# One two-column VectorE operation for a tile's guarded sum and the next tile's threshold, in an attention and two mixture-of-experts layers

## The chip, the cores and the metric

The kernel runs on one core of a Trainium2 chip. The metric is device microseconds of one execution. Engines are named as in the profile: PE is the matrix engine (PEld its weight loads), DVE is VectorE, ACT is ScalarE, POOL is GpSimd, SP issues most DMAs. Each engine runs its own instructions in the order in which they were written, and they meet through semaphores.

## The reference

Three layers follow each other, all in float32: an attention with a threshold (2 batches, 8 heads, 576 rows, 64 columns a head), and two mixture-of-experts layers over 1152 rows of 512, the first with 8 experts and a gate that is normalised over rows and columns in turn, the second with 4. Only the attention is touched here:

```python
scores = scale * np.matmul(q, k.transpose(0, 1, 3, 2))
thresh = np.max(scores, axis=-1, keepdims=True) - tau
scores = np.where(scores >= thresh, scores, -1000000000.0)
scores = scores - np.max(scores, axis=-1, keepdims=True)
attn = np.exp(scores)
attn = attn / (np.sum(attn, axis=-1, keepdims=True) + 1e-09)
return np.matmul(attn, v).astype(np.float32)
```

## The kernel before

The attention takes 72 tiles of 128 query rows by 576 keys, one after the other, in the first 232 us. Beside them PE computes the first two experts for the rows that are ready, matrix products written into the gaps ("fills", `expert_fill`), and ACT and POOL split their weights into a high and a low part (`cook`). The rest of the program, the other experts and the second layer, follows without a gap. A value written "fp32r" is the high or the low part of such a split.

What happens to a tile `u`, in the order of its life:

- `scores`: PE writes 128x576 scores into PSUM (`sc`, two buffers).
- `top`: DVE takes the largest of each row over the 576 (L287), 128x1, into column 0 of a small SBUF tile `st` (8 columns, six buffers); it stores the negative of it except in the first four tiles.
- `line`: the threshold, largest minus tau, into column 2. Three forms: the first four tiles do it with two DVE operations (L297, L298); the other twelve of the first sixteen (`exact`, products in full float32) with one DVE operation (L295); the remaining 56 with one ACT operation on 128x1 (L292).
- `exp`: ACT takes exp(score - largest) of the whole tile, PSUM to SBUF (L305).
- `mask`: one DVE operation multiplies by (score >= threshold) and sums the row into column 3 (L309; the sum is read out by a second short instruction).
- `guard`: DVE adds 1e-9 to the sum, 128x1 (L313).
- `norm`: DVE takes the reciprocal (L317) and POOL multiplies the tile by it in SBUF (L319).
- `turn`, `hi`, `lo`: PE transposes the tile (L327), ACT copies the high part out (L334, L336), DVE subtracts for the low part (L349, L352); then PE multiplies by v (L374, L376).

`step` writes the program. One call serves several tiles at different ages: `a` is the tile whose scores are ready, `d` the one before it, `x` one two tiles older than `d`. On DVE a step of the 56 reads: mask of `d`, top of `a`, guard of `d`, reciprocal of `d`, low part of `x`, further low parts (L401 of a finished head, L536 of a fill). On ACT: high part of `x`, exp of `a`, threshold of `a`, then the fill's activation (L533) and splits. So the threshold of `a` stands behind its exp on ACT, and the next step's mask waits for it. POOL's program has the norm of `d` (L319), the splits of keys, queries, values and finished heads (L85, L253, L254, L257) and a weight tile (L109).

The order is fixed by the program text: no scheduler moves an instruction. The number of fill products in a step is fixed too.

Of the kernel before, what the change touches and what calls it, by code (L numbers as in the profile page):

```python
# [9 lines left out]
F32 = mybir.dt.float32  # L10
F32R = mybir.dt.float32r
AF = mybir.ActivationFunctionType
ALU = mybir.AluOpType
AX = mybir.AxisListType
# [5 lines left out]
P = 128  # L20
# [3 lines left out]
HS = S // 2  # L24
# [5 lines left out]
def attention_two_moe_kernel(ctx, tc, qP, kP, qT, kT, vp, tau, wg, w1, w1s, w2, w2s, dp, m2w1s, m2w2, m2w2s, out):  # L30
    nc = tc.nc
    V, A, G, T = nc.vector, nc.scalar, nc.gpsimd, nc.tensor
# [24 lines left out]
    esc = cp.tile([P, 1], F32, name="esc")  # L57
    lin = cp.tile([P, 2], F32, name="lin")
    on = cp.tile([P, 2], F32, name="on")
# [32 lines left out]
    def fetch(n):  # L92
        while len(raws) < n and tiles:
            w, e, ft = tiles.pop(0)
            raw = rp.tile([P, DM], F32, tag="raw", name="raw", bufs=3)
            nc.sync.dma_start(raw, w[e, :, ft])
            raws.append(raw)
# [16 lines left out]
    class Expert:  # L114


        def __init__(self, i):
            self.w1 = lambda ft: cooked[2 * FT * i + ft]
            self.w2 = lambda ft: cooked[2 * FT * i + FT + ft]


    class Attention:
# [5 lines left out]
        def __init__(self, pl, ps_s, ps_t, ps_r, ps_m):  # L128
            self.pl, self.ps_s, self.ps_t, self.ps_r, self.ps_m = pl, ps_s, ps_t, ps_r, ps_m
            self.units, self.heads = [], []  # L130
            self.t = -2
            self.work = {}
            self.later, self.late = [], []
            self.iq = self.iv = self.lq = self.lv = 0
            self.xf = {}
            self.eth = pl.tile([P, 5, 640], F32R, name="eth")
            self.e32 = pl.tile([P, 5, 512], F32, tag="etl", name="e32")
            self.etl = None
            self.qz = [pl.tile([P, 3 * D], F32R, name=f"qz{i}") for i in range(2)]
            for z in self.qz:  # L140
                V.tensor_scalar(z[:, D:2 * D], ident[:, :D], 0.0, None, op0=ALU.mult)
# [141 lines left out]
                             start=i == 0, stop=i == len(ops) - 1)  # L283

        def top(self, u):
            st = u["st"] = self.pl.tile([P, 8], F32, tag="st", name="st", bufs=6)
            V.tensor_reduce(st[:, 0:1], u["sc"][:, :, :HS], axis=AX.XY, op=ALU.max, negate=not u["q"][0][0]["ws"])  # L287

        def line(self, u):
            st = u["st"]  # L290
            if not u["q"][0][0]["exact"]:
                A.activation(st[:, 2:3], st[:, 0:1], AF.Identity, bias=on[:, 1:2], scale=-1.0)  # L292
                return
            if not u["q"][0][0]["ws"]:
                V.tensor_scalar(st[:, 2:3], st[:, 0:1], -1.0, on[:, 0:1], op0=ALU.mult, op1=ALU.subtract)  # L295
                return
            V.tensor_scalar(st[:, 1:2], st[:, 0:1], lin[:, 0:1], None, op0=ALU.mult)  # L297
            V.tensor_scalar(st[:, 2:3], st[:, 0:1], lin[:, 1:2], None, op0=ALU.subtract)  # L298

        def exp(self, u):  # L300
            ex = u["ex"] = self.pl.tile([P, 2, HS], F32, tag="ex", name="ex", bufs=4)
            if u["q"][0][0]["ws"]:
                A.activation(ex, u["sc"][:, :, :HS], AF.Exp, bias=u["st"][:, 1:2], scale=esc)
            else:
                A.activation(ex, u["sc"][:, :, :HS], AF.Exp, bias=u["st"][:, 0:1])  # L305

        def mask(self, u):
            st, ex = u["st"], u["ex"]
            V.scalar_tensor_tensor(ex, u["sc"][:, :, :HS], st[:, 2:3], ex, op0=ALU.is_ge, op1=ALU.mult,  # L309
                                   accum_out=st[:, 3:4])  # L310

        def guard(self, u):
            V.tensor_scalar(u["st"][:, 4:5], u["st"][:, 3:4], 1e-9, None, op0=ALU.add)  # L313

        def norm(self, u):
            st = u["st"]
            V.reciprocal(st[:, 5:6], st[:, 4:5])  # L317
            exf = u["exf"] = u["ex"].rearrange("p a b -> p (a b)")
            G.tensor_scalar(exf, exf, st[:, 5:6], 1.0, op0=ALU.mult, op1=ALU.mult)  # L319

        def turn(self, u):
            eg, exf = u["eg"], u["exf"]
# [94 lines left out]
        def flush(self):  # L417
            self.run(self.later)
            self.run(self.late)

        def step(self, fill, side):

            us, t = self.units, self.t
            un = lambda i: us[i] if 0 <= i < len(us) else None
            self.load()
            nxt, a, d, x, c, z, y = (un(t + i) for i in (2, 1, 0, -2, -3, -4, -5))
            if x:
                self.turn(x)
            if d:
                self.mask(d)  # L430
            if a:
                self.top(a)
            if d:
                self.guard(d)
            if a and a["q"][0][0]["exact"]:
                self.line(a)
            if d:
                self.norm(d)
            for part, u in ((2, y), (1, z), (0, c)):
                for g in u["mix"] if u else ():  # L440
                    if g["head"]["exact"]:
                        self.mix(g, part)
            end = t > len(us)
            if x and not end:
                self.hi(x)
            for u, late in ((z, False), (y, True)):
                for g in u["mix"] if u else ():
                    if late == g["head"]["exact"]:
                        self.out(g)
            if end:  # L450
                self.run(self.later)
            if x and end:
                self.hi(x)
            if a:
                self.exp(a)
                if not a["q"][0][0]["exact"]:
                    self.line(a)
            fill(0, bool(c and c["mix"]))
            if x:
                self.lo(x)  # L460
            if nxt:
                self.scores(nxt)
            self.run(self.later)
            for g in c["mix"] if c else ():
                if not g["head"]["exact"]:
                    self.mix(g, 0)
            for w in self.work.pop(t, ()):
                w()
            fill(1, bool(c and c["mix"] or z and z["mix"]))
            self.run(self.late)  # L470
            side()
            self.t += 1
            return self.t < len(us) + 5
# [111 lines left out]
    with ExitStack() as att:  # L585
# [5 lines left out]
        at = Attention(ap, ps_s, ps_t, ps_r, ps)  # L591
# [20 lines left out]
        def side():  # L612
            if at.t >= -1:
                fetch(2)
            if at.t >= nA0 - 3 and raws and room[0] and (at.t % 3 < 2 if at.t < nA1 else room[0] > 2 or at.t % 2):
                room[0] -= 1
                cook()
            if at.t == 20:
                nc.sync.dma_start(wg_sb, wg)
                nc.sync.dma_start(dp_sb, dp)  # L620
            if at.t == 24:
                split(V, V, wg2[:, :, :E1], wg2[:, :, E1:], wg_sb)
# [962 lines left out]
```

## Time and profile before

| | |
|---|---|
| time, median of 3 runs | 1287.21 us (1286.96 to 1287.28) |
| the profiled execution | 1287.24 us, of it span 1285.5 us |
| busy: PE, DVE, ACT, POOL | 1268.6, 878.0, 738.0, 897.4 us |
| attention | first 232 us of the span |

Busy time is summed over the span; in the attention the engines take turns in being the last, so the part on the change is read from that stage alone. "Idle before, releaser" behind a row is how long the engine stood idle and whose end let it go on.

### The profile page before, as it was taken

What the parts mean: (1) busy time and instruction counts of PE and PEld (TensorE: products, weight loads), DVE (VectorE), ACT (ScalarE), POOL (GpSimd) and SP (SyncE); (2) the same over time, 40 slices, a digit from 0 to 9 for tenths busy, and PEclk for the clock granted to TensorE, in tenths of its full rate; (3) what the DMA queues carried; (4) which work ended last, traced back from release to release, by engine and by line L of the source; (5) the groups of instructions that cost most, each with busy time, mean ns of one, the idle gap of its engine ahead of it and who ended that gap; (6) DMA issues with size and microseconds to landing.
All of it is one profiled execution on the core that took longest, in us unless ns stands there. A gap on an engine that the chain in (4) does not pass through costs nothing.

```text
span 1285.5 us, 25112 instructions
## 1 busy us (share of the span) xinstructions
PE 1268.6 (99%) x9373; PEld 1209.0 (94%) x9373; DVE 878.0 (68%) x1843; ACT 738.0 (57%) x1491; POOL 897.4 (70%) x987
## 2 busy tenths in 40 slices
PE   8998999999999999999999999999999999999998
PEld 5597988889889999999999999999989999999998
DVE  6798888566637666666666666666745666666667
ACT  7887887423546555554655555466546465556552
POOL 7997987415796767867676786767668578677760
PEclk9999999999999999999999999999999999999999
DMA  5542330101221112211111221111212012111102
GB/s 170 162 126 77 97 98 17 42 1 34 81 67 50 42 42 58 58 34 51 50 42 42 58 59 34 50 50 42 58 38 62 17 53 57 35 55 50 42 18 74
DMA packets 43226, 73.84 MB, mean 57 GB/s; under 512 B 5217, under 2 KB 12513, under 8 KB 43105
## 3 DMA queue, kind: packets, MB, share of 16 engines
q1 hardware_dynamic: 42816, 71.96, 19.6%
q8 instruction: 74, 1.21, 0.4%
q14 instruction: 48, 0.39, 0.1%
q10 hardware_dynamic: 288, 0.28, 0.1%
HBM read 69.86 MB, written 2.36 MB: 56 GB/s over the span
## 4 chain that ended last, share of the span: by engine, by line
PE 89%; DVE 6%; ACT 2%; POOL 1%; issue 1%; DMA 1%; SPq 0%; DVEq 0%; POOLq 0%; ACTq 0%
PE mm L1123 36%; PE mm L1435 33%; PE mm L555 5%; PE mm L527 4%; PE mm L1243 3%; PE mm L282 2%; PE mm L327 2%; DVE ex L309 1%; PE mm L367 1%; DVE st L287 1%; PE mm L376 1%; DVE etl L349 1%; PE mm L374 1%; ACT ex L305 0%; DVE hl L536 0%
## 5 line engine op out<-in xcount | busy, mean ns | idle before, releaser
L85 POOL TENSOR_TENSOR wl<-raw,wh 128x512 fp32r<-128x512 f32 x217 | 282.9, 1310 | 180.2 <-ACT wh L80 166.9
L1223 DVE SCALAR_TENSOR_TENSOR acc<-mm,p,acc 128x256 f32<-128x256 f32 (+1 forms) x428 | 195.3, 508 | 72.5 <-PE mm L1435 59.6
L1435 PE MATMUL mm<-wh,h 128*128 128x256 f32 x960 | 173.6, 280 | 0.0
L1130 ACT COPY snap<-mm 128x576 f32<-128x576 f32 x126 | 80.8, 642 | 157.4 <-DVE mm L1284 77.8
L80 ACT CAST wh<-raw 128x512 fp32r<-128x512 f32 x217 | 133.4, 627 | 47.1 <-PE mm L1435 26.4
L1435 PEld LDWEIGHTS mm<-wh,h 128*128 128x128 f32 x960 | 146.7, 188 | 0.0
L1123 PE MATMUL mm<-xh,wl 128*128 128x288 f32 x672 | 146.3, 299 | 0.3
L1123 PE MATMUL mm<-xh,wh 128*128 128x288 f32 x672 | 143.6, 295 | 0.0
L1123 PE MATMUL mm<-xl,wh 128*128 128x288 f32 x672 | 143.1, 294 | 0.0
L1435 PE MATMUL mm<-wl,h 128*128 128x256 f32 x480 | 134.8, 281 | 0.0
L1435 PE MATMUL mm<-wh,tails 128*128 128x256 f32 x696 | 126.4, 280 | 0.0
L85 POOL TENSOR_TENSOR wl<-sum,wh 128x512 fp32r<-128x512 f32 x82 | 107.0, 1305 | 8.1 <-ACT wh L80 8.1
L1123 PEld LDWEIGHTS mm<-xh,wl 128*128 128x128 f32 x672 | 106.4, 188 | 2.8 <-DVE mm L1143 0.5
L1123 PE MATMUL mm<-xth,wl 128*128 128x288 f32 x504 | 108.3, 296 | 0.1
L1123 PEld LDWEIGHTS mm<-xl,wh 128*128 128x128 f32 x672 | 107.9, 188 | 0.0
L1123 PEld LDWEIGHTS mm<-xh,wh 128*128 128x128 f32 x672 | 107.8, 188 | 0.0
L1123 PE MATMUL mm<-xtl,wh 128*128 128x288 f32 x504 | 107.8, 295 | 0.0
L1123 PE MATMUL mm<-xth,wh 128*128 128x288 f32 x504 | 107.7, 295 | 0.0
L1435 PEld LDWEIGHTS mm<-wh,tails 128*128 128x128 f32 x696 | 106.3, 188 | 0.0
L80 ACT CAST wh<-sum 128x512 fp32r<-128x512 f32 x82 | 51.5, 628 | 85.4 <-POOL sum L820 71.9
L1435 PE MATMUL mm<-wl,tails 128*128 128x256 f32 x348 | 97.4, 280 | 0.0
L1435 PEld LDWEIGHTS mm<-wl,h 128*128 128x128 f32 x480 | 90.3, 188 | 0.4
(242 smaller groups left out, 3489.5 us busy)
## 6 DMA issues: line engine op xcount, KB each, us to landing
raw<-in_w1s SPq DMA_DIRECT2D x56, 256.0 KB, 2.7
raw<-in_w2s SPq DMA_DIRECT2D x48, 256.0 KB, 2.6
raw<-in_w SPq DMA_DIRECT2D x40, 256.0 KB, 3.1
raw<-in_m2w1s SPq DMA_DIRECT2D x32, 256.0 KB, 2.7
raw<-in_m2w2s SPq DMA_DIRECT2D x28, 256.0 KB, 2.6
kr<-in_kT SPq DMA_DIRECT2D x22, 288.0 KB, 3.0
vr<-in_vp SPq DMA_DIRECT2D x24, 160.0 KB, 2.3
qr<-in_qT SPq DMA_DIRECT2D x8, 288.0 KB, 2.9
```

The lines of the kernel that those rows point to most:

```text
L80: A.copy(hi, src)
L85: el.tensor_tensor(lo, src, f(hi), op=ALU.subtract)
L282: T.matmul(sc[:m, hf, :HS], lhsT=q, rhs=kk[:, hf * HS:(hf + 1) * HS], start=i == 0, stop=i == len(ops) - 1)
L287: V.tensor_reduce(st[:, 0:1], u["sc"][:, :, :HS], axis=AX.XY, op=ALU.max, negate=not u["q"][0][0]["ws"])
L327: T.transpose(et[:, kt], exf[:, kt * P:(kt + 1) * P], ident)
L527: T.matmul(ph[:, :n], lhsT=a[:, kt * P:(kt + 1) * P], rhs=x[:, kt, n0:n0 + n], start=i == 0 and kt == 0, stop=i == 2 and kt == KT - 1)
L555: T.matmul(py, lhsT=x, rhs=a, start=i == 0, stop=i == 3 * FT - 1)
L1123: T.matmul(ch[b][:, g, :HS], lhsT=w[:, (2 * g + kt) * P:(2 * g + kt + 1) * P], rhs=operand(u, kt, lo), start=first and j == 0, stop=j == l ...
L1130: A.copy(v[u], m)
L1223: V.scalar_tensor_tensor(a, src, s, a, op0=ALU.mult, op1=ALU.add)
L1243: T.matmul(py, lhsT=hid[x][:, kk, o:o + P], rhs=w[y], start=n == 0, stop=n == 3 * HF - 1)
L1435: T.matmul(m, lhsT=hid(x, kt + ko), rhs=wk[y], start=first and n == 0, stop=n == 5, skip_group_check=True)
```

## The change

The tile `st` with its six buffers of 8 columns goes, and one tile `sums` of six slots by 8 columns comes, which a step uses by turns. Its columns are laid out so that a step's two small subtractions stand side by side: columns 0 and 1 hold the sum of `d` and the constant tau term, columns 2 and 3 hold -1e-9 and the negated largest of `a`, and one tensor_tensor subtracts the second pair from the first into columns 4 (the guarded sum) and 5 (the threshold). Column 2 is filled once by a POOL memset, column 1 once by a DVE operation in step 0. The operation takes the place of `guard` and `line` in 68 steps: the 56 in which `line` was on ACT and the 12 in which it was a second DVE operation. The first four tiles keep their two operations, and the last step has a guard alone.

```diff
+            self.sums = pl.tile([P, 6, 8], F32, name="sums")
+            G.memset(self.sums[:, :, 2], -1e-9)
...
         def top(self, u):
-            st = u["st"] = self.pl.tile([P, 8], F32, tag="st", name="st", bufs=6)
-            V.tensor_reduce(st[:, 0:1], u["sc"][:, :, :HS], axis=AX.XY, op=ALU.max, negate=not u["q"][0][0]["ws"])
+            s = self.sums[:, (self.t + 6) % 6]
+            u["max"], u["line"] = s[:, 3:4], s[:, 5:6]
+            V.tensor_reduce(u["max"], u["sc"][:, :, :HS], axis=AX.XY, op=ALU.max, negate=not u["q"][0][0]["ws"])
...
-            if not u["q"][0][0]["exact"]:
-                A.activation(st[:, 2:3], st[:, 0:1], AF.Identity, bias=on[:, 1:2], scale=-1.0)
-                return
-            if not u["q"][0][0]["ws"]:
-                V.tensor_scalar(st[:, 2:3], st[:, 0:1], -1.0, on[:, 0:1], op0=ALU.mult, op1=ALU.subtract)
-                return
...
+            else:
+                V.tensor_tensor(s[:, 4:6], s[:, 0:2], s[:, 2:4], op=ALU.subtract)
...
         def mask(self, u):
...
+            V.scalar_tensor_tensor(ex, u["sc"][:, :, :HS], u["line"], ex, op0=ALU.is_ge, op1=ALU.mult,
+                                   accum_out=self.sums[:, self.t % 6, 0:1])
-        def guard(self, u):
-            V.tensor_scalar(u["st"][:, 4:5], u["st"][:, 3:4], 1e-9, None, op0=ALU.add)
...
             if a:
                 self.top(a)
-            if d:
-                self.guard(d)
-            if a and a["q"][0][0]["exact"]:
-                self.line(a)
+            self.line(a, d)
             if d:
                 self.norm(d)
...
             if a:
                 self.exp(a)
-                if not a["q"][0][0]["exact"]:
-                    self.line(a)
...
+            if at.t == 0:
+                V.tensor_scalar(at.sums[:, :, 1], at.sums[:, :, 2], 0.0, on[:, 1:2], op0=ALU.mult, op1=ALU.add)
```

DVE's program around 100 us into the execution, before: a tile's top, the guard and reciprocal of the tile ahead of it, a low part, the mask (`mm` is PSUM, `ex` the exp tile, `etl` the low part).

```order
L287 TENSOR_REDUCE st_1349<-mm_95 128x1 [waits PE_49]
L313 TENSOR_SCALAR st_1321<-st_1321 128x1 [waits DVE_49]
L317 RECIPROCAL st_1321<-st_1321 128x1 [waits DVE_49]
L349 TENSOR_TENSOR etl_986<-mm_95,eth_113 128x4x128 [waits Activation_49]
L309 SCALAR_TENSOR_TENSOR ex_1355,st_1349<-mm_95,st_1349,ex_1355 128x576 [waits Activation_49,Pool_49]
L287 TENSOR_REDUCE st_1397<-mm_95 128x1 [waits PE_49]
```

The same place in DVE's program with the change.

```order
L290 TENSOR_REDUCE sums_115<-mm_95 128x1 [waits PE_49]
L304 TENSOR_TENSOR sums_115<-sums_115 128x2 [waits DVE_49]
L320 RECIPROCAL sums_115<-sums_115 128x1 [waits DVE_49]
L352 TENSOR_TENSOR etl_943<-mm_95,eth_113 128x4x128 [waits Activation_49]
L315 SCALAR_TENSOR_TENSOR ex_1297,sums_115<-mm_95,sums_115,ex_1297 128x576 [waits Activation_49]
L290 TENSOR_REDUCE sums_115<-mm_95 128x1 [waits PE_49]
```

No instruction changes its place on DVE; the one-column operation on the sum of the tile ahead has become a two-column one that also reads what the operation right in front of it writes, and the mask waits on one semaphore where it waited on two.

ACT's program at the same place before: two tiles' exps, each with its threshold behind it, and what stands between.

```order
L305 ACTIVATE ex_1328<-mm_95,st_1321 128x576 [waits DVE_49,Pool_49]
L292 ACTIVATE st_1321<-st_1321,on_82 128x1
L334 CAST eth_113<-mm_95 128x4x128 [waits DVE_49,PE_49]
L305 ACTIVATE ex_1355<-mm_95,st_1349 128x576 [waits DVE_49,Pool_49]
L292 ACTIVATE st_1349<-st_1349,on_82 128x1
L80 CAST vhl_1382<-vr_1066 128x5x64 [waits DMAHW7_49,Activation_49]
```

And with the change.

```order
L311 ACTIVATE ex_1272<-mm_95,sums_115 128x576 [waits DVE_49,Pool_49]
L337 CAST eth_113<-mm_95 128x4x128 [waits DVE_49,PE_49]
L311 ACTIVATE ex_1297<-mm_95,sums_115 128x576 [waits DVE_49,Pool_49]
L80 CAST vhl_1323<-vr_1021 128x5x64 [waits DMAHW7_49,Activation_49]
L80 CAST kh_1326<-kr_1168 128x576 [waits DMAHW3_49,PE_49,Activation_49]
```

The threshold is gone from ACT and nothing else has moved; PE's and POOL's programs stand as before, but for POOL's one memset ahead of the first tile.

## Rows read from the trace of the kernel before

**Rows 1.** Windows: stretch, then busy us (and count) by engine, clock, DMA share.

```profile
46.00:71.10 25.10, 24.57 (x148) 17.43 (x149) 19.97 (x55) 21.41 (x48) 24.29 (x29) 1.00 0.55 155
71.10:98.28 27.18, 25.44 (x188) 23.68 (x187) 24.61 (x64) 22.75 (x54) 25.05 (x31) 1.00 0.44 125
127.80:178.20 50.40, 50.40 (x343) 47.69 (x344) 44.29 (x113) 39.87 (x87) 45.56 (x76) 1.00 0.33 93
...
240.00:1285.40 1045.40, 1040.73 (x7927) 1016.21 (x7925) 680.90 (x1313) 549.93 (x1084) 705.90 (x730) 1.00 0.17 48
```

**Rows 2.** Waits of DVE, 46 to 232 us: us in total, times, longest.

```profile
DVE hl L536 <- ACT hh L533: 6.7, 16, 0.5
DVE ex L309 <- ACT st L292: 6.2, 17, 0.9
DVE etl L349 <- ACT eth L334: 5.9, 8, 1.2
```

**Rows 3.** Chain that ended last, in order of time: start, us, piece.

```profile
71.10 0.28 ACT st L292
...
76.76 0.17 DVE st L317
...
223.93 0.29 ACT st L292
...
228.79 0.16 DVE st L317
```

**Rows 4.** Timeline of DVE, 115 to 118 us: start, us, operation, idle before.

```profile
115.39 0.75 DVE L287 TENSOR_REDUCE st<-mm 128x1 f32<-128x576 f32 x1
116.06 0.15 DVE L313 TENSOR_SCALAR st<-st 128x1 f32<-128x1 f32 x1
116.24 0.17 DVE L317 RECIPROCAL st<-st 128x1 f32<-128x1 f32 x1
116.32 0.67 DVE L349 TENSOR_TENSOR etl<-mm,eth 128x512 fp32r<-128x512 f32 x1
117.26 0.82 DVE L309 SCALAR_TENSOR_TENSOR ex<-mm,st,ex 128x576 f32<-128x576 f32 x1 [0.27 <-ACT st L292]
```

**Rows 5.** Timeline of ACT in the same step.

```profile
116.23 0.74 ACT L305 ACTIVATE ex<-mm,st 128x576 f32<-128x576 f32 x1 [0.81 <-DVE st L313]
116.87 0.28 ACT L292 ACTIVATE st<-st,on 128x1 f32<-128x1 f32 x1
117.06 0.45 ACT L80 CAST vhl<-vr 128x320 fp32r<-128x320 f32 x1
```

**Rows 6.** Timeline of DVE, 4 to 7 us, ahead of the first tiles.

```profile
4.93 0.16 DVE L609 TENSOR_TENSOR on<-tau_sb,on 128x1 f32<-128x1 f32 x1
...
6.00 0.76 DVE L287 TENSOR_REDUCE st<-mm 128x1 f32<-128x576 f32 x1 [0.73 <-PE mm L275]
6.79 0.21 DVE L297 TENSOR_SCALAR st<-st,lin 128x1 f32<-128x1 f32 x1
```

**Rows 7.** Timelines of DVE and POOL, 281 to 291 us, after the attention.

```profile
281.54 0.45 DVE L953 TENSOR_TENSOR sums<-sums 128x288 f32<-128x288 f32 x1
...
289.60 0.93 DVE L953 TENSOR_TENSOR sums<-sums 128x288 f32<-128x288 f32 x1
...
288.92 1.29 POOL L820 TENSOR_TENSOR raw<-sum,raw 128x512 f32<-128x512 f32 x1
```

**Rows 8.** Timelines of DVE and POOL, 78 to 80 us.

```profile
78.71 0.69 DVE L85 TENSOR_TENSOR wg<-wg_sb,wg 128x32 fp32r<-128x32 f32 x1
...
78.61 0.75 POOL L319 TENSOR_SCALAR ex<-ex,st 128x576 f32<-128x576 f32 x1
```

**Rows 9.** Groups of POOL by shape, 46 to 232 us: count, busy, mean ns, idle before.

```profile
L319 POOL TENSOR_SCALAR ex<-ex,st 128x576 f32<-128x576 f32 x59 | 44.0, 747 | 10.9 <-DVE st L317 10.4 <-PE mm L282 0.3
L109 POOL TENSOR_TENSOR wl<-raw,wh 128x512 fp32r<-128x512 f32 x25 | 32.3, 1291 | 0.0
L85 POOL TENSOR_TENSOR kl<-kr,kh 128x576 fp32r<-128x576 f32 x15 | 21.4, 1428 | 4.0 <-ACT kh L80 4.0
```

More of the change, by code (lines that the diff above doesn't have):

```diff
@@ L285, in top, with line @@
         def top(self, u):
-            st = u["st"] = self.pl.tile([P, 8], F32, tag="st", name="st", bufs=6)
-            V.tensor_reduce(st[:, 0:1], u["sc"][:, :, :HS], axis=AX.XY, op=ALU.max, negate=not u["q"][0][0]["ws"])
-        def line(self, u):
-            st = u["st"]
-            if not u["q"][0][0]["exact"]:
-                A.activation(st[:, 2:3], st[:, 0:1], AF.Identity, bias=on[:, 1:2], scale=-1.0)
-                return
-            if not u["q"][0][0]["ws"]:
-                V.tensor_scalar(st[:, 2:3], st[:, 0:1], -1.0, on[:, 0:1], op0=ALU.mult, op1=ALU.subtract)
-                return
-            V.tensor_scalar(st[:, 1:2], st[:, 0:1], lin[:, 0:1], None, op0=ALU.mult)
-            V.tensor_scalar(st[:, 2:3], st[:, 0:1], lin[:, 1:2], None, op0=ALU.subtract)
+            s = self.sums[:, (self.t + 6) % 6]
+            u["max"], u["line"] = s[:, 3:4], s[:, 5:6]
+            V.tensor_reduce(u["max"], u["sc"][:, :, :HS], axis=AX.XY, op=ALU.max, negate=not u["q"][0][0]["ws"])
+        def line(self, u, d):
+            s = self.sums[:, (self.t + 6) % 6]
+            ws = u and u["q"][0][0]["ws"]
+            if ws or not u:
+                if d:
+                    V.tensor_scalar(s[:, 4:5], s[:, 0:1], 1e-9, None, op0=ALU.add)
+                if ws:
+                    u["bias"] = s[:, 7:8]
+                    V.tensor_scalar(u["bias"], u["max"], lin[:, 0:1], None, op0=ALU.mult)
+                    V.tensor_scalar(u["line"], u["max"], lin[:, 1:2], None, op0=ALU.subtract)
+            else:
+                V.tensor_tensor(s[:, 4:6], s[:, 0:2], s[:, 2:4], op=ALU.subtract)
         def exp(self, u):
@@ L302, in exp @@
             if u["q"][0][0]["ws"]:
-                A.activation(ex, u["sc"][:, :, :HS], AF.Exp, bias=u["st"][:, 1:2], scale=esc)
+                A.activation(ex, u["sc"][:, :, :HS], AF.Exp, bias=u["bias"], scale=esc)
             else:
-                A.activation(ex, u["sc"][:, :, :HS], AF.Exp, bias=u["st"][:, 0:1])
+                A.activation(ex, u["sc"][:, :, :HS], AF.Exp, bias=u["max"])
         def mask(self, u):
-            st, ex = u["st"], u["ex"]
-            V.scalar_tensor_tensor(ex, u["sc"][:, :, :HS], st[:, 2:3], ex, op0=ALU.is_ge, op1=ALU.mult,
-                                   accum_out=st[:, 3:4])
-        def guard(self, u):
-            V.tensor_scalar(u["st"][:, 4:5], u["st"][:, 3:4], 1e-9, None, op0=ALU.add)
+            ex = u["ex"]
+            V.scalar_tensor_tensor(ex, u["sc"][:, :, :HS], u["line"], ex, op0=ALU.is_ge, op1=ALU.mult,
+                                   accum_out=self.sums[:, self.t % 6, 0:1])
         def norm(self, u):
-            st = u["st"]
-            V.reciprocal(st[:, 5:6], st[:, 4:5])
+            s = self.sums[:, self.t % 6]
+            V.reciprocal(s[:, 6:7], s[:, 4:5])
             exf = u["exf"] = u["ex"].rearrange("p a b -> p (a b)")
-            G.tensor_scalar(exf, exf, st[:, 5:6], 1.0, op0=ALU.mult, op1=ALU.mult)
+            G.tensor_scalar(exf, exf, s[:, 6:7], 1.0, op0=ALU.mult, op1=ALU.mult)
         def turn(self, u):
```

## The prediction

> **What bounds the kernel now.** I read the windows first. From 240 us on PE is busy for 1040.7 of 1045.4 us [rows 1] and nothing there is edited, so whatever the attention gains or loses moves the end by as much. Inside the attention PE is full from 127.8 to 178.2 us, but from 71.1 to 98.3 us it is busy for only 25.4 of 27.2 [rows 1]: there something else paces the program. POOL is the busiest or nearly so all along: 24.3 of 25.1 us from 46 us on, then 25.1 of 27.2, then 45.6 of 50.4 [rows 1]. Next I read who DVE waits for: the mask waits 17 times for the threshold on ACT, 6.2 us, and the fill's low part L536 waits 16 times, 6.7 us, for an activation that stands behind the threshold on ACT [rows 2]. The chain of waits tells which of these cost time. Between 46 and 232 us it runs through the threshold on ACT in 14 pieces, the first at 71.1 and the last at 223.9 us, and through the reciprocal on DVE in 11, from 76.8 to 228.8 us [rows 3]. So in about 25 of the 56 steps DVE and ACT set the pace; in the 14 DVE waits for ACT, in the 11 it works without a pause. The other steps are paced by PE, or around 46 to 71 us by POOL.
>
> **What leaves ACT.** 56 thresholds of 0.28 us. The next ACT operation starts 0.19 us after the threshold, because operations overlap (116.87 to 117.06) [rows 5]. That is the gain for L536 on a chain piece. For a mask it is more: without the threshold it follows the exp, which ends at 116.97 (116.23 and 0.74), instead of 117.26 [rows 4, 5], at most 0.29. On ACT's side the 14 pieces are worth 14 x 0.19 = 2.7 us or somewhat more. ACT elsewhere has idle time, and there it is worth nothing.
>
> **What comes to DVE: the dependency.** The guard needs only the old sum, so it starts 0.67 us after the top's start, before the top ends (115.39 and 0.75 is 116.14; guard at 116.06); 0.18 later comes the reciprocal, 0.08 later the low part [rows 4]. The new operation reads the largest that the top has just written. L297 does that at the program's start: it comes 0.79 us after the top's start, 0.03 after its end [rows 6]. A tensor_tensor on one column takes 0.16 us [rows 6]; the reciprocal then comes 0.16 + 0.03 = 0.19 later. So the low part starts 0.79 + 0.19 + 0.08 = 1.06 us after the top's start, where it was 0.93: **+0.13 us** on DVE in each step.
> The Trainium skill, page VectorE: DVE Perf Modes, section The DRAIN you can't avoid, says that the next operation waits for the pipe to empty in any case and that a semaphore costs nothing on top. By that the dependency is free and the sum below is 11 x 0.13 = 1.4 us smaller. The overlap of guard and top above speaks against it, and the rows decide.
>
> **What comes to DVE: the port.** This is the larger term, and the one I chose. The guard reads one tensor. The new operation reads two, both in SBUF. No DVE operation of the attention's steps does that: mask, top and the low parts take one input from PSUM. Where the trace has such operations, they stretch while POOL runs. L953 on 288 columns takes 0.45 us at 281.54; the same one at 289.60 takes 0.93, with a POOL operation from 288.92 to 290.21 beside it, and it ends 0.32 us after that one [rows 7]. Closer to this case, a 128x32 subtraction sits once between two steps: it takes 0.69 us from 78.71 to 79.40, and POOL's norm runs from 78.61 to 79.36 [rows 8]. It seems to stand until POOL's operation is through and to end 0.04 us behind it. No row shows two columns. The bounds are nothing (it slips through, 0.16 us) and the rest of a whole POOL operation, up to 1.43 us [rows 9]. I take the nearest row, the 32 columns: blocked, and done 0.04 us after POOL.
> The Trainium skill, page SBUF — State Buffer, section Who interferes with whom, speaks against this change in so many words: a VectorE instruction with two SBUF inputs contends with a GpSimd instruction that reads SBUF, and the one that comes second is fully blocked for the whole instruction. The trace agrees for 288 and 32 columns; by that rule width does not matter, and without it the sum below is that of the first rival.
> How long is such a wait? If the operation falls at any time of the 186 us from 46 to 232, the mean rest of a POOL operation is count x duration squared / 2, over 186. The three groups of rows 9 give 59 x 0.28 + 25 x 0.83 + 15 x 1.02 = 52.6, or 0.28 us. From each wait 0.12 us goes off, as the operation would take 0.16 anyway and ends 0.04 after POOL; the groups cover 97.7 us, 0.53 of the time, so 0.22 remains. They leave out POOL's smaller instructions, and POOL is busy for 0.90 to 0.97 of the stretches [rows 1], so I take **0.30 us a step**. A step then costs DVE 0.13 + 0.30 = 0.43 us.
>
> **Sum.** (1) The 11 pieces in which DVE works without a pause: 11 x 0.43 = +4.7. (2) The 14 pieces through ACT: DVE's own path had on average 6.2 / 17 = 0.36 us of idle before the mask and 6.7 / 16 = 0.42 before L536 [rows 2]. With 0.43 more it catches up with ACT's gain: the mean of both is about zero, and because the later of two ends counts and the waits scatter, I put +0.08 each, +1.1. (3) The mask waits on one semaphore where it waited on two. It starts 0.11 us after the threshold's end [rows 4, 5], which bounds that at 0 to 0.11 on DVE's pieces; I take -0.4 in all. (4) From 46 to 71 us POOL paces the program. A blocked operation is released when POOL's ends, and if POOL's next is the norm, it stands until the reciprocal is through (0.03 + 0.16 and some): 0 to 0.28 on 8 steps, I take half, +1.2. (5) Where PE paces, some 21 steps, DVE has slack (5.9 us in eight waits for the transposes' copies [rows 2]) against 0.43 a step, less what ACT gives back: between 0 and 9, and I take +1.0, as the slack lies in few places and long waits do not fit into the others. Together +7.6.
> At nothing I cost: the 12 full-float32 tiles, where one operation takes the place of two and DVE then waits for the exp (without that cover 12 x 0.43 = 5.2); POOL's memset and DVE's one-time fill, which stand beside the wait for the first data and for an exp (0.2 us each, uncovered); and a shift of the staging tiles in SBUF by the 192 bytes of `sums`, which no row prices. No DMA and no queue of SP is moved. Behind the waiting operation on DVE stand the reciprocal, for which POOL's norm waits, and the low parts, for which PE's products wait.
> The sum is made on the profiled execution, 1287.24 us, 0.03 above the median: 1287.24 + 7.6 = **1294.8 us**.
>
> **The rivals.**
> *Not slower: two columns slip past POOL.* Then DVE's step costs 0.13: 11 x 0.13 = 1.4, less 2.7, less 0.4, is -1.7, so 1285.5 us. For it speaks that no row has an operation so short; against it that the 32 columns were held as long as any. It decides on DVE's wait: with a mean under 0.13 us a step, 11 x (0.13 + 0.13) = 2.9 is met by 2.7 and 0.4, and the kernel is not slower.
> *The wait is absorbed.* The operation is blocked, but in the first 11 pieces it mostly finds POOL between operations, or POOL and DVE fall into step: half of (1), nothing of (4) and (5): 2.4 + 1.1 - 0.4 = +3.1 at the most, +1.5 in the middle, 1288.7 us. For it: POOL waits 10.4 us for reciprocals [rows 9], where nothing of POOL is in the way. Against it: POOL's busy share.
> *DVE becomes the bound everywhere.* All 56 steps pay 0.43, less 14 x 0.36 of idle and 2.7 us that ACT gives: 24.1 - 5.0 - 2.7 = +16.4, 1303.6 us. For it: from 127.8 to 178.2 us DVE is busy for 44.3 of 50.4 us; against it, that is still 0.4 us of room a step in 15 steps.
>
> **How the numbers follow.** A measurement of this kernel tells about 0.2%, 2.6 us, from no change. Forecast 0.70, nearly all of it slower than 1289.8. Slips past: 0.13, of which 0.05 is faster than 1284.6. Absorbed: 0.10, of which 0.08 is within 0.2%. Bound everywhere: 0.07. Faster 0.05, same 0.18, slower 0.77. The range goes from 1286.0, where some 0.08 of the first rival is left below, to 1301.0, with 0.10 left above; the forecast alone spans 1290 to 1301, its terms (1), (4) and (5) at their ends.
>
> **What would show it.** In the profile after, the new 128x2 operation should have a least duration of 0.16 us and a mean near 0.45, the long ones ending just after a POOL operation; its start should be 0.79 us after the top's, against 0.67 for the guard. The mask's waits for ACT should shrink, the chain should hold more DVE and POOL than now, and PE's busy share from 71 to 98 us should fall. After 240 us all should be as before, only later. If the operation never exceeds 0.2 us, the port step is wrong and the first rival holds. If it does and the attention is not longer, the sum of (1) and (2) is wrong.

## The result and the profile after

The changed kernel takes 1298.6 us (median of 6 runs, 1297.6 to 1298.79) against 1287.11 us for the kernel before on the same chip (6 runs, 1286.89 to 1287.28): a ratio of 1.0087, 95% interval 1.0076 to 1.0098, 11.5 us slower. The forecast was 1294.8 us, 7.6 us slower, in a range of 1286.0 to 1301.0. The side was right, the size two thirds of what came. The profiled execution of after is 1298.63 us with a span of 1296.8, where the span before was 1285.5: the two traces differ by 11.3 us, and that is what has to be found.

First the page of after: busy us and share of each engine, and then the chain of waits, its shares by engine, after and, below it, before.

```profile
PE 1270.8 (98%) x9373; PEld 1208.2 (93%) x9373; DVE 904.9 (70%) x1832; ACT 729.2 (56%) x1435; POOL 897.4 (69%) x988
```

```profile
PE 82%; DVE 10%; POOL 3%; ACT 2%; issue 2%; DMA 0%; DVEq 0%; POOLq 0%; ACTq 0%
```

```profile
PE 89%; DVE 6%; ACT 2%; POOL 1%; issue 1%; DMA 1%; SPq 0%; DVEq 0%; POOLq 0%; ACTq 0%
```

DVE is busy 26.9 us longer (878.0 before), though the change gives it one operation for one in the 56 steps and one for two in the 12 full-float32 tiles; ACT is 8.8 us less busy. In the chain DVE has 10% where it had 6, POOL 3 where it had 1. Next the same stretches as in [rows 1]: busy us and count of PE, PEld, DVE, ACT, POOL, then clock and DMA.

```profile
46.00:71.10 25.10, 24.28 (x143) 16.66 (x144) 22.94 (x56) 20.49 (x41) 24.20 (x31) 1.00 0.51 149
71.10:98.28 27.18, 25.71 (x192) 24.13 (x191) 26.19 (x63) 21.41 (x46) 25.06 (x30) 1.00 0.46 130
127.80:178.20 50.40, 45.47 (x309) 41.90 (x308) 47.96 (x102) 34.74 (x68) 42.21 (x72) 1.00 0.28 85
...
250.00:1296.70 1046.70, 1041.27 (x7930) 1016.10 (x7928) 680.77 (x1313) 549.82 (x1084) 706.19 (x731) 1.00 0.17 48
```

The gap opens late. From 127.8 to 178.2 us PE, full before (50.40), is busy for 45.47 us, and DVE, which had 6 us of room, has 2.4. From 46 to 98 us DVE is busier by even more (4.6 us against 3.7), and PE loses nothing: 49.99 us in the two stretches, 50.01 before. After 250 us PE works as it did, but for about 0.8 us.

The operation that does it, over the whole span of after: group, count, then busy us, mean ns of one, idle us before it.

```profile
L304 DVE TENSOR_TENSOR sums<-sums 128x2 f32<-128x2 f32 x68 | 34.4, 505 | 2.3
```

DVE's timeline in after (start, us, operation): the fill of the constant column, one step in which the operation is free, and the longest.

```profile
9.81 1.33 DVE L614 TENSOR_SCALAR sums<-sums,on 128x6 f32<-128x6 f32 x1
...
116.51 0.75 DVE L290 TENSOR_REDUCE sums<-mm 128x1 f32<-128x576 f32 x1
117.30 0.16 DVE L304 TENSOR_TENSOR sums<-sums 128x2 f32<-128x2 f32 x1
117.49 0.17 DVE L320 RECIPROCAL sums<-sums 128x1 f32<-128x1 f32 x1
117.57 0.67 DVE L352 TENSOR_TENSOR etl<-mm,eth 128x512 fp32r<-128x512 f32 x1
...
165.12 3.39 DVE L304 TENSOR_TENSOR sums<-sums 128x2 f32<-128x2 f32 x1
168.55 0.16 DVE L320 RECIPROCAL sums<-sums 128x1 f32<-128x1 f32 x1
```

POOL's timeline beside the fill and beside the longest:

```profile
9.71 1.41 POOL L85 TENSOR_TENSOR kl<-kr,kh 128x576 fp32r<-128x576 f32 x1
...
163.86 1.30 POOL L109 TENSOR_TENSOR wl<-raw,wh 128x512 fp32r<-128x512 f32 x1
165.13 0.76 POOL L322 TENSOR_SCALAR ex<-ex,sums 128x576 f32<-128x576 f32 x1
165.84 1.43 POOL L85 TENSOR_TENSOR kl<-kr,kh 128x576 fp32r<-128x576 f32 x1
167.23 1.27 POOL L109 TENSOR_TENSOR wl<-raw,wh 128x512 fp32r<-128x512 f32 x1
168.91 0.74 POOL L322 TENSOR_SCALAR ex<-ex,sums 128x576 f32<-128x576 f32 x1 [0.41 <-DVE sums L320]
```

Alone, at 117.30, the subtraction takes 0.16 us. At 165.12 it takes 3.39: three of POOL's operations pass, and it ends at 168.51, 0.01 after the last of them (167.23 and 1.27). Of the 68, 43 take more than 0.20 us, and 42 of these end 0.01 to 0.02 us after the end of a POOL operation. That POOL is what they stand behind rests on these ends; no run here takes POOL's work away. Over their least time the 68 stand 68 x (0.505 - 0.160) = 23.5 us; I call that the hold. DVE's waits of 6.2 us for the threshold and 6.7 for the fill's activation on ACT [rows 2] are all but gone; its waits in after, 46 to 244 us (us in total, times, longest):

```profile
DVE etl L352 <- ACT eth L337: 2.9, 5, 0.9
DVE ex L315 <- ACT ex L311: 1.0, 3, 0.5
DVE hl L534 <- ACT hh L531: 0.7, 4, 0.2
```

**Where the 11.3 us come from.** A mask starts each step on DVE; the start of the n-th mask after, less that of the n-th before, is how far the program is behind. The last row puts the forecast's terms (1), (2), (4) and (5) where their pieces stood; (3), -0.4, is left out.

| mask started before at, us | 16.3 | 44.3 | 68.1 | 129.5 | 220.3 | 229.8 |
|---|---|---|---|---|---|---|
| behind, after | 0.36 | 1.16 | 0.56 | 1.21 | 10.30 | 10.00 |
| behind, by the forecast's terms | 0 | 0 | 1.2 | 4.5 | 7.1 | 8.0 |

So 9.1 us are lost between 129.5 and 220.3 us, and next to nothing from 44 to 129. The loss from there on follows, for the most part, single holds. DVE's timeline in after, two long holds ahead of 129 us and one behind it:

```profile
55.45 1.20 DVE L304 TENSOR_TENSOR sums<-sums 128x2 f32<-128x2 f32 x1
103.66 1.13 DVE L304 TENSOR_TENSOR sums<-sums 128x2 f32<-128x2 f32 x1
...
135.92 1.43 DVE L304 TENSOR_TENSOR sums<-sums 128x2 f32<-128x2 f32 x1
```

From the mask ahead of it to the mask behind it, the lag grows by 0.20 us over the first, 0.14 over the second, and 1.40 over the third. Over the longest, the 3.39 us at 165.12, it grows by 2.82, which is nearly a third of the 9.1. Most long holds behind 129 us pass on in this way, though not all: over the 1.25 us at 184.33 it grows by 0.07.

Then 0.35 more are lost until the first long run of products behind the attention, and 1.05 around 350 us, far behind the change. ACT's timeline there, in the kernel before:

```profile
349.44 0.62 ACT L80 CAST wh<-raw 128x512 fp32r<-128x512 f32 x1 [2.41 <-DMA raw<-in_w]
```

And in after:

```profile
360.99 0.62 ACT L80 CAST wh<-raw 128x512 fp32r<-128x512 f32 x1 [3.61 <-PE mm L1123]
```

This split of a weight comes 11.55 us later where its neighbours come 10.36 later, and PE then waits 0.8 us for a copy that stands behind it on ACT. Whether the weight's transfer was late or its buffer, the trace does not settle (before it names the transfer, after a product of PE). It seems not to come with the change as such: none of the traces of the twelve kernels below loses more than 0.2 us at this place. Two of the six runs of after, 1297.6 and 1297.83, are some 1 us shorter than the other four (1298.56 to 1298.79) and may be without it; they have no trace.

### The profile page after: what moved, and what is told of

The parts are those of the page before. It is cut to its first block, busy times and chain, and to the rows that moved or that the text cites. A ratio compares the mean times of both kernels' runs of the same rounds, so it can differ in the third digit from the quotient of the medians.

```text
span 1296.8 us, 25008 instructions
## 1 busy us (share of the span) xinstructions
PE 1270.8 (98%) x9373; PEld 1208.2 (93%) x9373; DVE 904.9 (70%) x1832; ACT 729.2 (56%) x1435; POOL 897.4 (69%) x988
## 3 DMA queue, kind: packets, MB, share of 16 engines
q8 instruction: 74, 1.21, 0.4%
## 4 chain that ended last, share of the span: by engine, by line
PE 82%; DVE 10%; POOL 3%; ACT 2%; issue 2%; DMA 0%; DVEq 0%; POOLq 0%; ACTq 0%
PE mm L1123 34%; PE mm L1435 33%; PE mm L553 4%; PE mm L525 4%; PE mm L1243 3%; DVE ex L315 2%; DVE sums L290 2%; DVE sums L304 1%; DVE etl L352 1%; PE mm L330 1%; PE mm L284 1%; POOL wl L85 1%; DVE hl L534 1%; ACT ex L311 1%; POOL wl L109 1%
```

## The experiments

My theory was the forecast's: the new operation reads two tensors in SBUF, for which it uses a port of POOL, and it stands while POOL works. The rivals were the dependency (guard, reciprocal and low part now wait for the largest) and simply one operation more on DVE in steps that have no room. All kernels were compared with the kernel before on the same chip, whose median over all these runs was 1286.8 to 1286.9 us.

**One input in place of two (one_in).**

```diff
-                V.tensor_tensor(s[:, 4:6], s[:, 0:2], s[:, 2:4], op=ALU.subtract)
+                V.tensor_scalar(s[:, 4:6], s[:, 0:4:3], 1e-9, None, op0=ALU.add)
```

> The changed kernel, with its two-column operation in the same place and with the same producers and consumers, but with one input tensor in SBUF (a constant is added to the sum and to the negated largest) in place of two; the thresholds that come out are not the reference's. Port theory: the operation is never held behind POOL, it takes 0.16 us each time, the 23.5 us of holding in the changed kernel's trace are gone, DVE pays 0.13 us a step for the dependency and ACT is rid of its threshold: about 1286 us (1284 to 1288). Dependency theory (the loss comes from waiting for the largest, ahead of guard, reciprocal and low part): the operation costs a step as much as before, 1294 us or more.

Measured: 1297.75 us, 1.0082 (1.0065 to 1.0099). **My theory fell**, or so it looked: with one input the operation is held just as well. Its group, 18 to 244 us:

```profile
L304 DVE TENSOR_SCALAR sums<-sums 128x2 f32<-128x2 f32 x68 | 35.0, 514 | 2.3
```

Its long cases end 0.02 to 0.04 us after a POOL operation, and the one at 165.47 takes 3.42 us.

**Two one-column operations (dve_two).**

```diff
-                V.tensor_tensor(s[:, 4:6], s[:, 0:2], s[:, 2:4], op=ALU.subtract)
+                if d:
+                    V.tensor_scalar(s[:, 4:5], s[:, 0:1], 1e-9, None, op0=ALU.add)
+                V.tensor_scalar(u["line"], u["max"], -1.0, on[:, 0:1], op0=ALU.mult, op1=ALU.subtract)
```

> The changed kernel with its two-column operation replaced by two operations of DVE on one column, each with one input tensor: guard, then threshold. The threshold has left ACT here too. Port theory: neither is held; the guard starts 0.67 us after the top again, the threshold adds some 0.2 us of DVE to a step, paid in the 25 steps or so that DVE and ACT pace, less what ACT gives back: 25 x 0.2 - 2.7 = +2.3, about 1289 us (1285 to 1291). If any threshold on DVE costs what the change cost, because DVE has no room in the steps from 128 to 224 us: 1295 us or more.

Measured: 1286.88 us, 0.9999 (0.999 to 1.0009), the time of the kernel before. So DVE does have room for the threshold. The groups of threshold and guard, 18 to 244 us:

```profile
L306 DVE TENSOR_SCALAR sums<-sums,on 128x1 f32<-128x1 f32 x68 | 14.6, 214 | 0.0
L305 DVE TENSOR_SCALAR sums<-sums 128x1 f32<-128x1 f32 x68 | 9.7, 143 | 0.0
```

Neither is ever held: the means are the least times. The reciprocal starts 0.92 us after the top's start (0.85 before, 0.97 at the least in the changed kernel), so a threshold on DVE costs 0.07 us a step, and at the last mask this kernel is 1.39 us ahead of the kernel before. That is what ACT gives back, less the 0.07 and less 0.30 lost at the start.

**An additional operation that nothing waits for (plus_tt, plus_ts).** Here the kernel before is left as it is, and one operation on a tile of its own is put behind the guard, with two inputs or with one:

```diff
+            if a and not a["q"][0][0]["exact"]:
+                V.tensor_tensor(self.pad[:, 4:6], self.pad[:, 0:2], self.pad[:, 2:4], op=ALU.subtract)
...
+                V.tensor_scalar(self.pad[:, 4:6], self.pad[:, 0:2], 1e-9, None, op0=ALU.add)
```

> The kernel before, with one more DVE operation in each of the 56 steps, behind the guard: a subtraction of two columns from two columns of a tile in SBUF that nothing else uses. Nothing waits for its result, ACT keeps its threshold. Port theory: it takes 0.16 us at least and about 0.5 us on average, the long ones end just behind a POOL operation, and the kernel is 8 to 14 us slower, 1295 to 1301 us. Dependency theory: it costs 0.16 us in the steps that DVE paces, 1289 to 1291 us.

> The same as the one with two inputs, but the additional operation adds a constant to two columns: one input tensor. Both theories: 0.15 us each, never held, at most 0.16 us in some 25 steps: 1287 to 1291 us. What the other one takes beyond this is the second input in SBUF alone.

Measured: 1297.92 us, 1.0082 (1.0067 to 1.0097), and 1297.73 us, 1.0081 (1.0066 to 1.0096). Two things follow. The dependency falls as the main cause: an operation that depends on nothing and that nothing depends on costs about as much as the whole change. The two totals are made up differently, though; the table of lags below shows it. And one input on two columns is held like two inputs; the expectation for plus_ts, 1287 to 1291, missed. The group of the additional operation in plus_tt:

```profile
L440 DVE TENSOR_TENSOR pad<-pad 128x2 f32<-128x2 f32 x56 | 30.0, 535 | 0.0
```

And in plus_ts:

```profile
L440 DVE TENSOR_SCALAR pad<-pad 128x2 f32<-128x2 f32 x56 | 30.3, 541 | 0.0
```

So far one-column operations with one input were free, two-column operations held with one input or two. Is it then the second column, and the second input nothing?

**One column: two inputs or one (plus_t1, plus_s1), and two columns with one of two inputs in PSUM (plus_tp).** The additional operation again, in three more forms:

```diff
+                V.tensor_tensor(self.pad[:, 4:5], self.pad[:, 0:1], self.pad[:, 2:3], op=ALU.subtract)
...
+                V.tensor_scalar(self.pad[:, 4:5], self.pad[:, 0:1], 1e-9, None, op0=ALU.add)
...
+                V.tensor_tensor(self.pad[:, 4:6], a["sc"][:, 0, 0:2], self.pad[:, 2:4], op=ALU.subtract)
```

> The kernel before with the additional two-column subtraction, but its first input is two columns of the next tile's scores in PSUM, so that one input alone is in SBUF. Three readings of what the additional operation with one input in SBUF showed (held all the same): (a) DVE takes a port that POOL also uses when an operation has two inputs in SBUF, and also when a one-input operation on more than one column runs from SBUF to SBUF in a faster mode; by that this one is free of it, 0.2 us each, never held, 1287 to 1290 us. (b) Any operation on two columns is held, or the additional operation costs by its place: 1297 to 1298 us.

> The kernel before with the additional subtraction on one column instead of two, both inputs in SBUF. If two inputs in SBUF are enough to be held, as (a) says and as the forecast took it: mean about 0.5 us, 1296 to 1298 us. If it is the second column alone that does it: 0.16 us each and 1287 to 1290 us, and the forecast was right for a wrong reason.

> The kernel before with an additional addition of a constant on one column, one input in SBUF, one output in SBUF. By (a) it is never held, 0.15 us each. The additional operation with an input in PSUM was not held either and cost 3 us; in its trace the exp of the next tile starts 0.91 us after its largest begins to be taken, in place of 0.78, because the additional operation reads the same scores in PSUM. If that later exp was its price, this one costs little: 1286.5 to 1288 us. If any further DVE operation costs 3 us: 1289.5 to 1290.5 us.

Measured: plus_t1 1297.75 us, 1.0085 (1.007 to 1.0101); plus_s1 1287.98 us, 1.0008 (0.9999 to 1.0017); plus_tp 1290.0 us, 1.0027 (1.0017 to 1.0038). The group of the additional operation, in plus_t1:

```profile
L440 DVE TENSOR_TENSOR pad<-pad 128x1 f32<-128x1 f32 x56 | 29.8, 533 | 0.0
```

In plus_s1:

```profile
L440 DVE TENSOR_SCALAR pad<-pad 128x1 f32<-128x1 f32 x56 | 8.0, 144 | 0.0
```

In plus_tp:

```profile
L440 DVE TENSOR_TENSOR pad<-mm,pad 128x2 f32<-128x2 f32 x56 | 8.3, 148 | 0.0
```

Reading (a) holds in all five forms. Two inputs in SBUF are enough, on a single column. One input is enough on two columns, from SBUF to SBUF. One input on one column, or a second input in PSUM, is free. Between the two one-column forms everything but the second input is the same: that input costs 29.8 - 8.0 = 21.8 us of DVE and 9.8 us of the kernel.
The Trainium skill has both ways: page SBUF — State Buffer, section Who interferes with whom, counts a tensor_scalar that enters a two-port mode among what contends with GpSimd, beside operations with two SBUF inputs, and page VectorE: DVE Perf Modes, section What auto-detection actually checks, says that a single-source operation takes such a mode if source and destination are in SBUF and their outermost non-unit dimensions are both even or equal. Two columns are, one column has none; the runs agree with both rules, 541 against 144 ns.

plus_tp is not held and yet costs 3 us. Its timeline of DVE, the top and the additional operation of one step:

```profile
113.51 0.75 DVE L289 TENSOR_REDUCE st<-mm 128x1 f32<-128x576 f32 x1
...
114.24 0.15 DVE L440 TENSOR_TENSOR pad<-mm,pad 128x2 f32<-128x2 f32 x1
```

And of ACT, the exp that follows:

```profile
114.48 0.74 ACT L307 ACTIVATE ex<-mm,st 128x576 f32<-128x576 f32 x1 [0.26 <-DVE pad L440]
```

The exp starts 0.97 us after the top's start (113.51 to 114.48), and so in nearly all steps in which ACT stood idle; in the kernel before it is 0.84 (115.39 to 116.23) [rows 4, 5]. The trace names the additional operation, which reads the same scores in PSUM, as what it waited for. plus_s1, without that, costs 1.2 us, inside its measurement's 0.2%.

**The change without the hold (one_psum, one_col).** The changed kernel, its operation in place, with its first input in PSUM, or as one one-column operation that takes the largest as a scalar of each partition:

```diff
-                V.tensor_tensor(s[:, 4:6], s[:, 0:2], s[:, 2:4], op=ALU.subtract)
+                V.tensor_tensor(s[:, 4:6], u["sc"][:, 0, 0:2], s[:, 2:4], op=ALU.subtract)
...
-                V.tensor_tensor(s[:, 4:6], s[:, 0:2], s[:, 2:4], op=ALU.subtract)
+                u["line"] = s[:, 4:5]
+                V.tensor_scalar(s[:, 4:5], s[:, 0:1], s[:, 3:4], None, op0=ALU.add)
```

> The changed kernel, its two-column subtraction in place and with both columns written as before, but its first input is two scores in PSUM in place of the sum and the constant; what it computes is not the reference's. It still waits for the largest, the reciprocal and the masks still wait for it, ACT still has no threshold. If holding behind POOL is the whole loss: 0.16 to 0.2 us each, and what is left is the dependency's 0.13 us on 11 pieces against what ACT gives back, about 1286 us (1284 to 1288). If the dependency or the place costs too: 1290 us or more.

> The changed kernel with its two-column operation replaced by one one-column operation that adds the largest, as a scalar of each partition, to the sum; its one result goes to the reciprocal and to the next mask, so neither is the reference's. It waits for the same two producers and the same consumers wait for it, ACT has no threshold, nothing is read from PSUM. If the holding is all that the change costs and the dependency nothing: 1286 to 1287.5 us, as with two one-column operations. If waiting for the largest costs by itself: 1289 us, as with the input in PSUM.

Measured: 1288.96 us, 1.0017 (1.0008 to 1.0027), and 1288.48 us, 1.0014 (1.0005 to 1.0023). Both lie between what the two readings had expected. The subtraction in one_psum is never held, and the kernel is 2.2 us slower than the kernel before on its chip in place of 11.5, so 9.3 us are gone:

```profile
L304 DVE TENSOR_TENSOR sums<-mm,sums 128x2 f32<-128x2 f32 x68 | 10.8, 159 | 2.3
```

In the 2 us that are left the dependency is mixed with other things. In one_psum the exp starts 1.04 us after the top in place of 0.84, again because of the scores in PSUM. In one_col it starts as before, and the low part 1.12 us after the top (0.93 before, 1.05 at the least in the changed kernel); its ten runs fall into two groups, 1287.5 to 1287.7 and 1289.2 to 1290.2, and the profile, one of the second, has a stretch around 90 us in which POOL stood for 1.65 us with no cause that the trace names. In the first group, which has no trace, later guard and low part cost 0.8 us. So if the second group is put down to that stretch, which one trace alone cannot show, the dependency is worth about 1 us; it was not measured apart from the rest.

**Early and late (early_tt, late_tt).** The two-column operation only in the tiles up to the mask that starts at 131 us in the changed kernel (129.5 before), or only from there on; the others have dve_two's pair. The edit of early_tt, for which late_tt has `>=` and the other order:

```diff
-            else:
+            elif self.t < 42:
                 V.tensor_tensor(s[:, 4:6], s[:, 0:2], s[:, 2:4], op=ALU.subtract)
+            else:
+                if d:
+                    V.tensor_scalar(s[:, 4:5], s[:, 0:1], 1e-9, None, op0=ALU.add)
+                V.tensor_scalar(u["line"], u["max"], -1.0, on[:, 0:1], op0=ALU.mult, op1=ALU.subtract)
```

> The changed kernel with the two-column operation only from the tile whose mask starts at 134 us on; the tiles ahead of it have the two one-column operations of DVE instead. By the starts of the masks in the two traces (0.5 us of lag gained from 46 to 131 us, 9 from there to 224): nearly the whole loss stays, 1295 to 1298 us. By the terms of the forecast (5 of the 11 DVE pieces and 4 of the 14 ACT pieces lie there, and most of the PE-paced steps): about +3, 1290 us.

> The other half: the two-column operation only up to the tile whose mask starts at 131 us, two one-column operations of DVE from there on. If the cost of a hold depends on its place and the halves add up: 1298.6 - (1295.4 - 1286.9) = 1290.1 us, or less, as the later steps can take some lag back: 1287 to 1290. By the forecast's terms, of which more than half lay there: about 1292 us.

Measured: late 1295.39 us, 1.0067 (1.0052 to 1.0082); early 1287.91 us, 1.0008 (0.9999 to 1.0018). Late came out as the starts of the masks had told, and not as the forecast's terms had it (1290); for early the terms had said 1292. The same operation in 39 and in 29 steps costs 1.1 us in the one and 8.6 in the other. How far each kernel is behind the kernel before at a mask:

| mask started before at, us | 44.3 | 68.1 | 129.5 | 220.3 | 229.8 |
|---|---|---|---|---|---|
| changed | 1.16 | 0.56 | 1.21 | 10.30 | 10.00 |
| early_tt | 1.22 | 0.64 | 1.32 | 0.63 | 0.59 |
| late_tt | 0.29 | -0.33 | -0.70 | 8.31 | 8.01 |
| dve_two | 0.27 | -0.35 | -0.68 | -1.34 | -1.39 |
| plus_tt | 0.52 | 1.79 | 3.72 | 10.69 | 10.68 |

Against dve_two, the change without holds, early costs 0.59 + 1.39 = 1.98 and late 8.01 + 1.39 = 9.40 by the last mask: together 11.38, and the changed kernel 11.39. The halves add up. In the changed kernel's trace the holds are 5.9 us in 27 operations from 46 to 131 us, and 14.1 us in 27 from there to 231. What becomes of them is seen in windows (columns as above), first of the kernel before and, below it, of the changed kernel:

```profile
46.00:127.80 81.80, 76.52 (x500) 64.05 (x500) 70.71 (x183) 66.03 (x149) 69.83 (x85) 1.00 0.42 118
```

```profile
46.00:127.80 81.80, 76.67 (x500) 64.09 (x501) 77.25 (x182) 61.59 (x122) 70.42 (x86) 1.00 0.41 117
```

Then of late_tt:

```profile
127.80:178.20 50.40, 46.41 (x314) 42.88 (x313) 47.40 (x105) 35.05 (x68) 41.93 (x72) 1.00 0.30 88
```

Up to 128 us DVE's busy time rises by 6.5 us and PE's stays where it was: DVE had 11 us of idle there and takes the holds into it. In the stretch behind, late_tt loses 4 us of PE, where the changed kernel loses 5. The early stretch does not take in everything: plus_tt, in which ACT keeps its threshold and gives nothing back, has 8.6 us of holds from 46 to 131 us and falls behind by 3.2 us from 44.3 to 129.5.

**Without the guard (no_guard).** dve_two without the guard: the reciprocal reads the sum itself, and stands ahead of the threshold.

```diff
-                if d:
-                    V.tensor_scalar(s[:, 4:5], s[:, 0:1], 1e-9, None, op0=ALU.add)
                 V.tensor_scalar(u["line"], u["max"], -1.0, on[:, 0:1], op0=ALU.mult, op1=ALU.subtract)
...
-            V.reciprocal(s[:, 6:7], s[:, 4:5])
+            V.reciprocal(s[:, 6:7], s[:, 0:1])
...
-            self.line(a, d)
             if d:
                 self.norm(d)
+            self.line(a, d)
```

> The kernel with two one-column operations of DVE, without the guard: the 1e-9 that the reference adds to the sum of a tile's exponentials is left out (the largest score of a row gives exp of 0, so the sum is 1 or more, and in float32 it is the same number with or without it). The reciprocal comes right behind the largest, 0.67 us after its start in place of 0.85 in the kernel before, and the threshold behind the reciprocal. If DVE or the norm on POOL still paces some 11 steps: 11 x 0.18 = 2 us less, about 1285 us (1283.5 to 1286.5). If PE takes up whatever DVE gives back: 1287 us.

Measured: 1285.52 us, 0.999 (0.9981 to 0.9998). It is the shortest of all, 1.25 us below the kernel before on its chip, as the first of the two readings had it, and the interval only just leaves out no change. A step of its DVE, in which the reciprocal comes 0.67 us after the top:

```profile
114.88 0.75 DVE L290 TENSOR_REDUCE sums<-mm 128x1 f32<-128x576 f32 x1
115.55 0.15 DVE L318 RECIPROCAL sums<-sums 128x1 f32<-128x1 f32 x1
115.67 0.21 DVE L302 TENSOR_SCALAR sums<-sums,on 128x1 f32<-128x1 f32 x1
```

It rests on the largest of a row being kept by the threshold, as it is for any tau of zero or more.

## Why the prediction was right, and where it was not

**The port: right, and more than the forecast.** The operation was to have a least time of 0.16 us and a mean near 0.45, the long ones ending just behind a POOL operation. They are 0.16 and 0.505, and 42 of 43 long ones end 0.01 to 0.02 us behind one. plus_t1 against plus_s1 shows that the second input in SBUF does it. The reading from the nearest row, the 32 columns of [rows 8], carried over to two columns and to one; the first rival, that so short an operation slips past, is out.

**Its size: a little low.** 0.30 us a step was the forecast, worked out as if the operation fell at any time. In the 54 operations from 46 to 231 us the hold is (5.9 + 14.1) / 54 = 0.37. In the first 27 it is 0.22, what the three groups of [rows 9] alone had given, and in the last 27 it is 0.52, of which the one long hold at 165 us makes 0.12. From 131 us on the steps do not seem to fall at random: the operation comes again and again just behind the start of a long one of POOL (189.04 behind 188.88, 200.18 behind 200.10, both splits of 1.29 us).

**The dependency: its times right, its price not measured apart.** The operation starts 0.79 us after the top and the low part 1.05 at the earliest, as worked out (0.79 and 1.06). The forecast put 11 x 0.13 = 1.4 us on that; one_col's shorter runs leave about 1. plus_tt shows that the loss doesn't need it. The sentence of the Trainium skill that the prediction weighed, from The DRAIN you can't avoid on page VectorE: DVE Perf Modes, does not fit the traces as it stands alone: dve_two's guard still starts 0.67 us after the start of the top, which takes 0.75, and an operation that depends on the top not before 0.78. The same section goes on to say that a next operation which is not held starts earlier; the prediction left that out, and the guard's start agrees with it.

**ACT's part: right in direction.** DVE's waits for the threshold and the fill's activation are all but gone in the changed kernel, in part because DVE itself is later: in dve_two, without holds, the mask still waits 2.3 us for the exp and L536 3.2 for ACT. The gain was to be 2.7 us on the pieces through ACT, less what the later reciprocal takes. dve_two, which has that gain and no holds, is 1.4 us ahead at the last mask. At the end of the program 0.7 of it is left and the median is the same as before. Term (3), the one semaphore fewer, was not measured apart.

**The sum by place: wrong.** This is the step that failed. Terms (1) and (2) put a price of 0.43 and 0.08 us on the steps in which the chain of [rows 3] went through DVE and ACT, mostly ahead of 129 us: 3.3 us there, and 1.2 for (4). Measured from 44 to 129.5 us: from 1.16 to 1.21, nothing, or 1.0 against dve_two, which gains that much from ACT there. A chain that passes an operation says that this operation was last, not that a delay of 0.4 us has nowhere to go: windows give DVE 11 us of idle in 82 there, and 27 holds of 0.22 fit in. That ACT gives something back is part of it: plus_tt, without that, loses 3.2 us there. Term (5) put +1.0 on the steps that PE paced, since "the slack lies in few places"; its bounds were 0 and 9. From 129.5 to 220.3 us the loss is 9.1. There 0.13 + 0.52 us a step meet 0.4 us of room (6.1 us in 15 steps), and most long holds pass on to the mask behind them, so DVE becomes the bound, as the third rival had it for all 56 steps; the second, that the wait is absorbed, is what happened ahead of that. Two errors of opposite sign, -4.5 us from 44 to 129.5 and +6.5 from there to 220.3, with +1.2 ahead of them and -1.2 behind, left the terms 2 us short at the last mask. That the total came as near as it did is luck; the mechanism of the hold was right, its price by place was not.
With this went one of the signs: PE's share from 71 to 98 us was to fall, and it rose a little, 25.44 to 25.71 us; it fell from 127.8 to 178.2.

**Costed at nothing: not all of it was.** The fill of the constant column, priced at 0.2 us if uncovered, took 1.33: one input, six columns, held until POOL's split of 9.71 us ended at 11.12. The second mask starts 0.38 us later, and dve_two, which keeps the fill, is 0.30 behind from there. The full-float32 tiles cost 0.8 us of lag (0.36 to 1.16) with 3.5 us of holds in 11 operations, where dve_two has nothing; DVE's wait for the exp covers most of it, not all. Behind the attention everything was to be as before, only later; it is, but for the 1.05 us at 350 us in the profiled run.

**The sum against the span, then:** 10.0 us at the last mask, 0.35 up to the end of the attention, 1.05 behind it make 11.4; the spans differ by 11.3.

## What to carry to other kernels

Two short operations on two engines are not made cheaper by one instruction if that one has to stand until another engine's operation ends: here 0.14 us of DVE and 0.28 of ACT became 0.51 of DVE. Keep the small bookkeeping on DVE to one input and one column while POOL works in SBUF, or to two inputs of which one is in PSUM (where that delays no other engine's read of the same tile), and look at the least and the longest time of a group before its mean. A price per step is not a loss per step: ask of each stretch how much idle time the delayed engine has, and by whom it is paced, and let a kernel with the operation in one half only tell.

## What the hardware showed that was not expected

- A one-input operation on two columns, SBUF to SBUF, is held as long as a two-input one: 541 against 535 ns on average, 144 on one column.
- A held operation is not always let in when POOL's next one begins. At about 165 us it stood past three POOL operations in the changed kernel (3.39 us), in one_in (3.42), plus_tt (3.20), plus_t1 (3.20), plus_ts (3.04) and late_tt (3.53), although nearly all others were let in at the first end of a POOL operation. In the changed kernel this one hold is followed by 2.82 of the 9.1 us lost. What sets it apart stays open.
- An operation that only reads scores in PSUM on DVE delayed an exp on ACT that reads the same scores, by 0.13 us in plus_tp and 0.20 in one_psum; the traces name the operation as what the exp waited for. Whether the chip needs that wait, no run here shows.
